# Moving the output stores of an attention kernel from SyncE's DMA queue to ScalarE's

## The chip, the cores and the metric

The kernel runs on one core of a Trainium2 chip. A core has five engines that run side by side and meet at semaphores: TensorE (matrix products), VectorE, ScalarE (activation functions such as exp), GpSimd and SyncE. Data moves between the chip's memory (HBM) and the on-chip memory (SBUF) by DMA, which the core's 16 DMA engines carry out. SyncE and ScalarE can each start transfers on a DMA queue of their own.

The metric is the time of one execution on the device in microseconds (us). Before the change it is 831.01 us, the median of three runs from 830.96 to 833.51 us.

## The reference

The kernel computes attention with a full softmax over 16 x 32 = 512 heads, each with 192 queries, 1024 keys and a head size of 128, in bf16:

```python
B, H, Sq, Sk, D = 16, 32, 192, 1024, 128
def reference(q, k, v):
    scale = q.shape[-1] ** -0.5
    scores = jnp.einsum("bhqd,bhkd->bhqk", q, k) * scale
    p = _softmax(scores, axis=-1)
    return jnp.einsum("bhqk,bhkd->bhqd", p, v)
```

The inputs are normal numbers times 0.05. K and V are 134 MB each, Q and the output 25 MB each.

## The kernel before, in words

**Groups and fills.** Four heads make a group x, of which there are NQ = 128. The scores of a group are worked on in three fills, so there are NF = 384 fills; fill f is part b = f mod 3 of group x = f // 3. In a fill TensorE makes transposed scores of all four heads into PSUM (`qk`, line 616): one bank for one head (`f_s2`) and a set of three banks for the other three (`f_s0` and `f_s1` in turn). ScalarE takes the exp of the one bank (line 782) and of the three (line 785), and writes bf16 probabilities to `f_pt`. The maximum isn't subtracted. The sum of the exps comes from a column of ones next to V.

**P times V.** Four fills later (LAG = 4) TensorE multiplies the probabilities by V (`pv`, line 638) into one PSUM bank, `f_o`. On VectorE `onorm` takes the reciprocal of the sums (line 722, which counts up the semaphore `s_rc`) and multiplies by it (line 726), which writes a third of a group's output to `f_ob`. As `f_o` is a single bank, the next `pv` waits for that multiplication (semaphore `s_on`).

**Loads.** For each group SyncE starts a load of V (line 517, 1024 KB), of K (line 503, 1024 KB) and of Q (line 509, 192 KB). There are five buffers of each. K and Q are transposed on VectorE (lines 701 and 710) and K is put in order on GpSimd (line 573); V is copied on GpSimd to lie beside its ones (line 582). A load of K waits until VectorE has transposed the group that had its buffer; a load of V waits for the P·V step past which its buffer is free.

**Stores.** The output of two groups is stored by one transfer of 384 KB in pieces of 768 B (line 529); the last two groups have one each. That makes 65 stores. The buffer `f_ob` has NSO = 3 slots of two groups, and VectorE's first multiplication into a slot waits until the slot's last store has landed (semaphores `s_st`). A store waits for the reciprocal after its last block's multiplication, which tells that the block is written.

**The order on SyncE.** The whole order is written out by hand in one loop over n: load V of group n+3, K and Q of group n+5, and then, for every second n, one store. SyncE works through it in order, so a store that has to wait holds back the loads behind it, and a load that has to wait, for its buffer or for room in the queue, holds back the store.

**ScalarE.** Its loop over the fills holds nothing but the waits and the two exps of each fill.

**A second path.** Behind the main path follows a general path that runs only if a check of the sums, made at the end, asks for it. It isn't entered with these inputs and is left as it is.

Of the kernel before, what the change touches and what calls it, by code (L numbers as in the profile page):

```python
# [408 lines left out]
def _attention_kernel(nc, q, k, v, out):  # L409
# [4 lines left out]
    NQ = NH // 4  # L414
# [4 lines left out]
    NF = 3 * NQ  # L419
# [4 lines left out]
    NSO = 3  # L424
# [5 lines left out]
    of = out.rearrange("b h s d -> (b h) s d")  # L430

    stores = [(x, GQ) for x in range(0, NQ - GQ, GQ)] + [(NQ - 2, 1), (NQ - 1, 1)]
    EARLY = NF - 9

    with ExitStack() as outer:
        redo = outer.enter_context(nc.sbuf_tensor("redo", [1, 1], mybir.dt.int32))

        def sem(name):
            return outer.enter_context(nc.semaphore(name))
# [7 lines left out]
        s_st = [sem("f_st%d" % i) for i in range(NSO)]  # L447
# [9 lines left out]
        s_rc = sem("f_rc")  # L457
        s_pf = sem("f_pf")
        s_on = sem("f_on")
        s_fin = sem("f_fin")  # L460
        s_fl = sem("f_fl")

        with ExitStack() as es:
            def sb(name, shape, dt):
                return es.enter_context(nc.sbuf_tensor(name, shape, dt))
# [16 lines left out]
            ob = sb("f_ob", [128, NSO, GQ * 6, D], BF16)  # L482
# [10 lines left out]
            def o_of(s):  # L493
                if NF - 4 <= s < NF - 1:
                    return s3_ps[0][:, s - (NF - 4), :].rearrange("p (u c) -> p u c", u=2)
                return o_ps[:]

            @block.sync
            def _(e):
                def load_k(x):  # L500
                    if x >= NKN:
                        e.wait_ge(s_kx, 3 * (x - NKN) + 3)
                    e.dma_start(
                        kn[:, x % NKN, :],
                        kf[4 * x:4 * x + 4].rearrange("a (j r) d -> (a j) (r d)", r=32).bitcast(U32),
                    ).then_inc(s_kn[x % NKN], 16)

                def load_q(x):
                    e.dma_start(
                        qn[:, x % NKN, :],  # L510
                        qf[4 * x:4 * x + 4].rearrange("a (j u) d -> (a j) (u d)", u=6).bitcast(U32),
                    ).then_inc(s_qn[x % NKN], 16)

                def load_v(x):
                    if x >= NVS:
                        e.wait_ge(s_pv, 3 * (x - NVS) + 2 + BLANK)
                    e.dma_start(
                        vs[:, x % NVS, :, :],
                        vf[4 * x:4 * x + 4].rearrange("a (m t) d -> m a (t d)", t=T),
                    ).then_inc(s_v[x % NVS], 16)  # L520

                def store(i):
                    so = i % NSO
                    x, c = stores[i]
                    if x + c == NQ:
                        e.wait_ge(s_fin, 1)
                    else:
                        e.wait_ge(s_rc, 3 * (x + c) + 1)
                    e.dma_start(
                        of[4 * x:4 * x + 4 * c].rearrange("(a x) (p j) d -> (x p) a (j d)", x=2, j=3),  # L530
                        ob[:, so, 0:6 * c, :].rearrange("p (a j) d -> p a (j d)", j=3),
                    ).then_inc(s_st[so], 16)

                k0 = kf[0:4].rearrange("a (j s t) d -> (a j) s (t d)", s=4, t=8).bitcast(U32)
                kn0 = kn[:, 0].rearrange("p (s w) -> p s w", s=4)
                cut = 32 * PIECES[0][1]
                e.dma_start(kn0[:, :, 0:cut], k0[:, :, 0:cut]).then_inc(s_k0, 16)
                load_q(0)
                e.dma_start(kn0[:, :, cut:], k0[:, :, cut:]).then_inc(s_kn[0], 16)
                load_k(1)  # L540
                load_q(1)
                for n in range(2, NKN):
                    load_v(n - 2)
                    load_k(n)
                    load_q(n)
                si = 0
                for n in range(NQ + 3):
                    if n + NKN - 2 < NQ:
                        load_v(n + NKN - 2)
                    if n + NKN < NQ:  # L550
                        load_k(n + NKN)
                        load_q(n + NKN)
                    if si < len(stores) - 2 and n >= sum(stores[si]) + 2:
                        store(si)
                        si += 1
                while si < len(stores):
                    store(si)
                    si += 1
                for so in range(NSO):
                    e.wait_ge(s_st[so], 16 * len(range(so, len(stores), NSO)))  # L560

# [209 lines left out]
            @block.scalar  # L771
            def _(act):
                act.wait_ge(s_one, 1)
                act.activation(pt[:, 1].rearrange("p a c -> p (a c)").bitcast(F32), ones[:, 0:1].to_broadcast([128, 2 * T * SQ]),  # L774
                               ACT_FN.Copy).then_inc(s_set, 1)
                for f in range(NF):
                    x, b = divmod(f, 3)
                    act.wait_ge(s_qk, f + 1)
                    if 0 < 3 * x + b and b < 2:
                        act.wait_ge(s_pv, 3 * (x - R) + 2 + b + BLANK)  # L780
                    c = slice(512 * b, 512 * b + 512)
                    act.activation(pt[:, x % R, 0, c], s1_ps[:], ACT_FN.Exp, scale=scale).then_inc(s_e1, 1)  # L782
                    if b == 0:
                        act.wait_ge(s_pf, x + 1)
                    act.activation(pt[:, x % R, 1:4, c], s3_ps[f % 2][:], ACT_FN.Exp, scale=scale).then_inc(s_e3, 1)  # L785

        _general_path(nc, q, k, v, out, redo)


def bass_standalone__mha_softmax__near_ridge_kernel(  # L790
    nc: bass.Bass,
    q: bass.AP,
    k: bass.AP,
    v: bass.AP,
    out: bass.AP,
):
    _attention_kernel(nc, q, k, v, out)
# [28 lines left out]
```

## Time and profile before

| Quantity | Value |
|---|---|
| time, median of 3 runs | 831.01 us |
| span of the profiled execution | 829.9 us |
| TensorE busy | 810.1 us (98%) |
| ScalarE busy | 748.5 us (90%), 384 exps of 1444 ns and 384 of 597 ns |
| VectorE busy | 601.8 us (73%) |
| GpSimd busy | 550.9 us (66%) |
| DMA | 319.21 MB, 385 GB/s over the span |
| time of the packets on SyncE's queue, share of 16 DMA engines | 100.6% |
| stores, from issue to landing (median) | 13.8 us |
| loads of K, V, Q, from issue to landing (median) | 14.2, 12.5, 12.9 us |

The profile is one execution seen by the hardware profiler. PE stands for TensorE, DVE for VectorE, ACT for ScalarE, POOL for GpSimd, SPq for the issuing of SyncE. An issue is the time in which the issuing engine hands a transfer over; its landing is when the data has arrived and the semaphore is up. In the timelines a line gives the start in us, the length in us, the engine, the line of the program and the operation, and in square brackets the idle time ahead of it with what ended it. Matmuls are pipelined, so a busy TensorE says only that it had work at all times.

### The profile page before, as it was taken

Reading aid. Unit: us, or ns where it says so; the run is one execution under the profiler, and the core shown is the slowest. Engines: PE = TensorE matmul, PEld = TensorE weight load, DVE = VectorE, ACT = ScalarE, POOL = GpSimd, SP = SyncE. Lnnn points to the kernel's source line nnn. Section 1 sums busy time; section 2 is a strip of 40 time slices with the busy share of each in tenths; the row PEclk is TensorE's granted clock in tenths of the full one; section 3 lists DMA queues with packets and bytes.
Section 4 is the critical chain, followed back from the end, with each engine's and each line's share of the span. In section 5 each row is a group of like instructions: output and inputs, shape, how many; then the busy total and the mean of one; then the engine's idle time right before and its main releaser. Section 6 shows DMA issues by size and latency. Waiting matters only on the chain. (4 is left out here: it accounts for less than half of the span.)

```text
span 829.9 us, 71554 instructions
## 1 busy us (share of the span) xinstructions
PE 810.1 (98%) x32926; PEld 718.3 (87%) x32926; DVE 601.8 (73%) x1288; ACT 748.5 (90%) x770; POOL 550.9 (66%) x646
## 2 busy tenths in 40 slices
PE   6899999999999999999999999999999999999995
PEld 4788888888888888888888888888888888888885
DVE  5477777777777777777777777777777777777763
ACT  5699999999999999999999999999989999999994
POOL 6566766766766766766766666666766666666671
PEclk9899999999999999999999999999999999999999
DMA  8999999999999999999999999999999999999981
GB/s 323 399 403 399 406 403 401 406 403 402 405 403 404 402 400 389 399 382 374 398 400 398 376 399 395 388 400 405 387 383 399 406 397 397 387 393 405 399 323 46
DMA packets 139214, 319.21 MB, mean 385 GB/s; under 512 B 7201, under 2 KB 57377, under 8 KB 122913
## 3 DMA queue, kind: packets, MB, share of 16 engines
q1 hardware_dynamic: 139168, 318.80, 100.6%
q14 instruction: 40, 0.32, 0.1%
q8 instruction: 6, 0.10, 0.1%
HBM read 293.60 MB, written 25.17 MB: 384 GB/s over the span
## 5 line engine op out<-in xcount | busy, mean ns | idle before, releaser
L785 ACT ACTIVATE f_pt<-f_s 128x1536 bf16<-128x1536 f32 x384 | 554.5, 1444 | 3.4 <-PE f_o L638 3.4
L573 POOL COPY f_kt<-f_kx 128x768 uint32<-128x768 uint32 (+1 forms) x384 | 294.2, 785 | 258.1 <-DVE f_kx L701 139.8
L638 PE MATMUL f_o<-f_vp,f_pt 128*64 128x129 bf16 x12336 | 424.9, 222 | 5.2 <-issue 3.3
L616 PE MATMUL f_s<-f_qt,f_kt 32*128 32x192 bf16 (+2 forms) x20480 | 422.2, 226 | 5.0 <-issue 3.2
L638 PEld LDWEIGHTS f_o<-f_vp,f_pt 128*64 128x64 bf16 x12336 | 366.1, 110 | 57.6 <-issue 28.3
L616 PEld LDWEIGHTS f_s<-f_qt,f_kt 32*128 32x128 bf16 x20480 | 347.8, 92 | 41.2 <-issue 5.5
L701 DVE STREAM_TRANSPOSE f_kx<-f_kn 128x768 uint32<-128x768 uint32 (+1 forms) x384 | 334.7, 872 | 32.0 <-DMA f_kn<-in_k_dram 30.2
L782 ACT ACTIVATE f_pt<-f_s 128x512 bf16<-128x512 f32 x384 | 229.3, 597 | 65.7 <-PE f_s L616 38.1
L582 POOL COPY f_vp<-f_vs 128x1024 uint32<-128x1024 uint32 x256 | 259.9, 1044 | 5.9 <-PE f_o L638 5.5
L722 DVE RECIPROCAL f_rinv<-f_o 128x2 f32<-128x2 f32 x381 | 64.3, 169 | 166.3 <-PE f_o L638 165.8
L726 DVE TENSOR_TENSOR f_ob<-f_o,f_rinv 128x256 bf16<-128x256 f32 x381 | 161.8, 425 | 19.7 <-DMA out_dram<-f_ob 7.1
L710 DVE STREAM_TRANSPOSE f_qt<-f_qn 128x384 uint32<-128x384 uint32 x128 | 72.9, 569 | 0.0
L663 PE MATMUL f_o<-f_ones 128*128 128x512 bf16 x12 | 5.3, 632 | 1.1 <-POOL f_ones L564 1.1
L663 PEld LDWEIGHTS f_o<-f_ones 128*128 128x128 bf16 x12 | 1.6, 144 | 3.8 <-issue 2.8
L565 POOL MEMSET f_vp<- 128x4352 uint32 x1 | 3.7, 3730 | 0.0
L682 DVE MEMSET f_pt<- 128x3072 uint32 x1 | 2.6, 2618 | 1.5 <-PEq L811 1.5
L638 PE MATMUL f_s<-f_vp,f_pt 128*64 128x129 bf16 x96 | 3.1, 220 | 0.3 <-PEq L599 0.3
L638 PEld LDWEIGHTS f_s<-f_vp,f_pt 128*64 128x64 bf16 x96 | 2.8, 110 | 0.5 <-issue 0.5
L774 ACT ACTIVATE f_pt<-f_ones 128x3072 f32<-128x3072 bf16 x1 | 2.8, 2762 | 0.0
L774 ACT ACT_TABLE_LOAD x1 | 1.3, 1283 | 0.8 <-PEq L811 0.8
L722 DVE RECIPROCAL f_rinv<-f_s 128x2 f32<-128x2 f32 x3 | 0.5, 170 | 1.4 <-PE f_s L638 1.4
L676 PE MATMUL f_o<-f_bad,f_ones 128*1 128x1 bf16 x1 | 0.2, 164 | 1.3 <-DVEq L766 1.3
(13 smaller groups left out, 5.3 us busy)
## 6 DMA issues: line engine op xcount, KB each, us to landing
f_vs<-in_v_dram SPq DMA_DIRECT2D x128, 1024.0 KB, 12.5
f_kn<-in_k_dram SPq DMA_DIRECT2D x127, 1024.0 KB, 14.2
f_qn<-in_q_dram SPq DMA_DIRECT2D x128, 192.0 KB, 12.9
out_dram<-f_ob SPq DMA_DIRECT2D x63, 384.0 KB, 13.8
f_kn<-in_k_dram SPq DMA_DIRECT2D x1, 640.0 KB, 6.6
f_kn<-in_k_dram SPq DMA_DIRECT2D x1, 384.0 KB, 4.0
out_dram<-f_ob SPq DMA_DIRECT2D x2, 192.0 KB, 2.0
```

The source lines that it names most:

```text
L573: gp.tensor_copy(kt[:, x % NKT].bitcast(U32).rearrange("p U (j s u) c -> p U j s (u c)", s=2, u=2)[:, lo:hi], kx[:, x % 2].rearrange("p (U ...
L582: gp.tensor_copy(vp[:, x % NVP, 2 * T * i: 2 * T * i + 2 * T, 0:D].bitcast(U32), vs[:, x % NVS, 2 * i: 2 * i + 2, :].rearrange("p a (t d) ...
L616: ins = pe.matmul(S[:, c0: c0 + n1 - n0], kt[r, x % NKT, 2 * t + h, :, c], qt[r, x % R, h, n0:n1, c], start=w == 0 and g == 0, stop=w == 3 ...
L638: return pe.matmul(O[m0: m0 + m, u, 0:129], pt[:, x % R, 2 * y + z, t * SQ + n0: t * SQ + n0 + m], vp[:, x % NVP, (2 * y + z) * T + t, 0:129],
L663: pe.matmul(o_ps[:].rearrange("p a b -> p (a b)"), ones[:], ones[:].unsqueeze(1).to_broadcast([128, 4, 128]), start=True, stop=True)
L701: dve.transpose(kx[:, x % 2].rearrange("p (U s j u) -> p s u U j", s=2, j=32, u=2)[:, :, :, lo:hi], kn[:, x % NKN].rearrange("p (s u U i) ...
L710: dve.transpose(qt[:, x % R].bitcast(U32).rearrange("p b (y j u) c -> p u y b (j c)", y=3, u=2), qn[:, x % NKN].rearrange("p (u y b i) -> ...
L722: dve.reciprocal(ri, O[:, :, 128]).then_inc(s_rc, 1)
L726: dve.tensor_tensor(ob[:, so, 6 * a + 2 * w: 6 * a + 2 * w + 2, :], O[:, :, 0:128], ri.unsqueeze(2).to_broadcast([128, 2, D]), ALU.mult,). ...
L774: act.activation(pt[:, 1].rearrange("p a c -> p (a c)").bitcast(F32), ones[:, 0:1].to_broadcast([128, 2 * T * SQ]), ACT_FN.Copy).then_inc( ...
L782: act.activation(pt[:, x % R, 0, c], s1_ps[:], ACT_FN.Exp, scale=scale).then_inc(s_e1, 1)
L785: act.activation(pt[:, x % R, 1:4, c], s3_ps[f % 2][:], ACT_FN.Exp, scale=scale).then_inc(s_e3, 1)
```

## The change

The function that starts a store moves out of SyncE's block, so that either engine can call it. ScalarE calls it right behind the second exp of fill 3(x+c)+6, where x is the first group of the store and c its number of groups. The last block of that store is block 3(x+c)-1, whose P·V product TensorE makes right after the scores of fill 3(x+c)+3; the reciprocal that the store waits for belongs to the following block, a fill later. The exp is two fills past that. Stores for which this fill doesn't exist, the last three, stay on SyncE, behind all its loads. SyncE's loop then holds loads only. The waits, the sizes and the slots stay as they were.

The change is meant to take the waits of stores out of the order of the loads, and the wait for a load's buffer out of the way of the stores.

```diff
+            def store(e, i):
+                so = i % NSO
+                x, c = stores[i]
+                if x + c == NQ:
+                    e.wait_ge(s_fin, 1)
+                else:
+                    e.wait_ge(s_rc, 3 * (x + c) + 1)
+                e.dma_start(
+                    of[4 * x:4 * x + 4 * c].rearrange("(a x) (p j) d -> (x p) a (j d)", x=2, j=3),
+                    ob[:, so, 0:6 * c, :].rearrange("p (a j) d -> p a (j d)", j=3),
+                ).then_inc(s_st[so], 16)
+
+            store_at = {3 * (x + c) + 6: i for i, (x, c) in enumerate(stores) if 3 * (x + c) + 6 < NF}
...
             @block.sync
...
-                si = 0
-                for n in range(NQ + 3):
+                for n in range(NQ):
                     if n + NKN - 2 < NQ:
                         load_v(n + NKN - 2)
                     if n + NKN < NQ:
                         load_k(n + NKN)
                         load_q(n + NKN)
-                    if si < len(stores) - 2 and n >= sum(stores[si]) + 2:
-                        store(si)
-                        si += 1
-                while si < len(stores):
-                    store(si)
-                    si += 1
+                for i in range(len(store_at), len(stores)):
+                    store(e, i)
...
             @block.scalar
...
                     act.activation(pt[:, x % R, 1:4, c], s3_ps[f % 2][:], ACT_FN.Exp, scale=scale).then_inc(s_e3, 1)
+                    if f in store_at:
+                        store(act, store_at[f])
```

More of the change, by code (lines that the diff above doesn't have):

```diff
@@ L520, in load_v @@
                     ).then_inc(s_v[x % NVS], 16)
[L522 to L532, printed above, removed]
                 k0 = kf[0:4].rearrange("a (j s t) d -> (a j) s (t d)", s=4, t=8).bitcast(U32)
```

## The prediction

> **What bounds the kernel now.** I read the page's shares first, then busy time by stretch, then the list of waits, and last the timelines of ScalarE, VectorE, TensorE and SyncE.
>
> The busy times by stretch (columns: busy time of PE, weight loads, DVE, ACT, POOL with counts, then clock, share of the DMA engines, GB/s):
>
> ```profile
> 45.00:535.00 490.00, 489.99 (x20206) 436.81 (x20204) 366.37 (x790) 458.80 (x474) 337.02 (x395) 1.00 1.04 397
> 535.00:800.00 265.00, 263.17 (x10792) 233.99 (x10782) 197.27 (x422) 244.87 (x254) 179.62 (x211) 1.00 1.04 396
> ```
>
> TensorE has no gap in the first stretch and 1.8 us of gaps in the second. The DMA engines are full in both. So two bounds lie almost on each other. In the ScalarE timeline the starts of L782 are 12.42 us apart over six fills (two groups of four heads), in every such stretch from fill 12 (44.72 us) to fill 252 (541.72 us) but two, and those lose 0.1 us each. From there on they are 12.45 to 13.13 us apart. Against fill by fill medians of the early part, fills 252 to 380 lose 3.5 us in all, and 3.0 of it falls on fills whose number leaves 5 when divided by 6: once per pair of groups, the rhythm of a store. What happens there, at its worst (start, length, engine, line):
>
> ```profile
> 600.38 2.24 SPq L529 DMA_DIRECT2D out_dram<-f_ob  x1
> 602.42 0.42 DVE L726 TENSOR_TENSOR f_ob<-f_o,f_rinv 128x256 bf16<-128x256 f32 x1 [0.86 <-DMA out_dram<-f_ob]
> 602.99 1.10 PE L638 MATMUL f_o<-f_vp,f_pt 128*64 128x129 bf16 x32 [0.61 <-PEq L599]
> 605.17 0.60 ACT L782 ACTIVATE f_pt<-f_s 128x512 bf16<-128x512 f32 x1 [0.81 <-PE f_s L616]
> ```
>
> VectorE wants to write an output slot whose previous store has not landed. It waits 0.86 us; TensorE's next P·V waits 0.61 us for the single output bank; the exp after it comes late. In the list of waits this is the second line:
>
> ```profile
> DVE f_kx L701 <- DMA f_kn<-in_k_dram: 30.2, 42, 3.6
> DVE f_ob L726 <- DMA out_dram<-f_ob: 7.1, 22, 0.9
> ```
>
> (us in total, how often, the longest). 6.7 us of the 7.1 lie between 535 and 800 us. K waits are there too, 17.6 us in 32 waits of at most 0.8 us:
>
> ```profile
> 544.08 0.98 DVE L701 STREAM_TRANSPOSE f_kx<-f_kn 128x768 uint32<-128x768 uint32 x1 [0.72 <-DMA f_kn<-in_k_dram]
> 544.98 0.13 DVE L722 RECIPROCAL f_rinv<-f_o 128x2 f32<-128x2 f32 x1
> ```
>
> They lengthen no fill yet, but the reciprocal behind this one shows no idle time, where it usually has some 0.55 us. VectorE's slack is used up by a K wait of 0.7 us.
>
> **Why late and not early.** SyncE issues every transfer, in order:
>
> ```profile
> 66.47 0.17 DVE L722 RECIPROCAL f_rinv<-f_o 128x2 f32<-128x2 f32 x1 [0.58 <-PE f_o L638]
> 70.64 0.55 SPq L529 DMA_DIRECT2D out_dram<-f_ob  x1
> 74.72 0.38 SPq L517 DMA_DIRECT2D f_vs<-in_v_dram  x1
> ...
> 501.48 3.47 SPq L517 DMA_DIRECT2D f_vs<-in_v_dram  x1
> 505.00 4.38 SPq L503 DMA_DIRECT2D f_kn<-in_k_dram  x1
> 509.41 0.43 SPq L509 DMA_DIRECT2D f_qn<-in_q_dram  x1
> ```
>
> At 71.19 us it has nothing to do for 3.5 us; at 500 us one issue follows on the other and some last over 4 us: the queue takes no more. Summing SyncE's gaps ahead of V loads over 0.2 us gives 38 us for 45 to 150, 13 us for 250 to 350 and none after 450. The lead melts because supply is below demand. A group needs 1024 + 1024 + 192 KB of loads and 192 KB of stores, 2.49 MB, in 6.21 us: 401 GB/s, against 397 supplied. The packet records of the trace show why: [...]768 B of a store in 36 ns, 2 KB of V in 86, 8 KB of K in 316 ns before 150 us and 336 between 350 and 535.
>
> **What the Trainium skill says.** "DMA: Bandwidth & Descriptors", section "Issuing engines are not separate DMA queues": transfers started by different engines run on the same 16 DMA engines and only issue time is saved. The trace agrees as far as it goes: the one queue already fills the engines (1.04). The same page, "Queues, rings and completion order": each DMA engine takes packets round robin from the rings that have work; so a store on a second ring overtakes queued loads. No run here shows it yet. "Perfetto Trace Analysis", section "DMA Instruction — HWDGE (DVE, Sync)": the descriptor generator is locked for one issuing engine until its descriptors are made, and others wait for the lock. The trace has one issuer, so it cannot show that. "Advanced Engine Details and Errata", section "Sequencer Loop": other engine instructions can be queued while a control instruction runs. That is what would hide an issue behind an exp; not shown here either.
>
> **The change, part by part.**
> 1. *62 of 65 stores leave SyncE.* The rule for the fill is 3(x+c)+6 < 384, so ends x+c = 2 to 124. SyncE saves 62 x 0.45 us = 28 us of issuing and the waits for the reciprocal (8.1 us between 150 and 535). It is worth nothing by itself: where SyncE has gaps nobody waits for it, and where it has none it waits for the DMA queue.
> 2. *62 issues on ScalarE.* An unhindered issue takes 0.43 us (median of the 231 SyncE issues under 0.7 us). Its semaphore wait is long over: the store in fill 186, whose first exp starts at 405.00 us, needs the reciprocal that ended at 402.08. Behind the issue is queued L782 of the next fill. ScalarE sends L785 off at 405.49, that exp lasts 1.44 us, and L782 starts at 407.05. So between 0 (hidden behind L785) and 62 x 0.43 = 27 us (if all of it came after the exp). ScalarE has only 0.12 to 0.17 us between L785 and the next L782, so what isn't hidden reaches TensorE. I take 0: 0.43 us fits three times into the exp.
> 3. *The stores land sooner.* Today 13.8 us from issue, the whole queue ahead. On its own ring at most about 32 packets an engine, each next to one load packet: 32 x (36 + 86) ns = 3.9 us beside V, 32 x (36 + 316) = 11.3 us beside K. From fill X+6 to the reuse of the slot at the P·V step X+12 are some ten fills, 20.7 us. The slot wait ends: 3.0 us of lost fills fall away.
> 4. *The bytes stay.* Without the slot waits TensorE asks for 401 GB/s where 397 came. Over the 265 us that is 265 x (401/397 - 1) = 2.7 us of lateness, and K has next to no slack left. If DMA stays exactly as quick, K waits take back up to 2.7 of the 3.0 us (gain 0.3 us: 830.7). If queue depth freed of stores carries the loads over the dips, all 3.0 stay (828.0). I take the middle, a gain of 1.5 us: **829.5 us**.
> 5. *The end.* The last three stores and the chain behind the last P·V stay on SyncE as they are: nothing.
>
> **The rivals.**
> - *TensorE alone bounds* (0.20): two rings interleave small store packets with the loads and the 8 KB packets keep their early 316 ns. Packets over 400 ns cost 12 us per engine over the run, so there is room. Then 371 fills after fill 12 take 371 x 2.07 = 768.0 instead of 771.7 us: 831.0 - 3.7 = 827.3. This is the floor, as the change leaves TensorE's work alone. For: early supply was 403. Against: nothing shown says that a second ring helps.
> - *ScalarE waits for the descriptor generator* (0.19): the issue comes while SyncE holds it. Laid over the SyncE timeline of before, 12 of the 62 places fall more than 1.5 us ahead of the end of a SyncE issue; the overhang is 29 us. Each stall slows the demand and lets SyncE out of its jam, so I estimate a third to a half: 831 - 1.5 + 12 = 841 us, at worst 860. For: SyncE is issuing for 722 us of the span. Against: a separate queue may have its own room.
> - *The mix makes DMA slower* (0.13): with 1% less, 745 us need 401/393 - 1 = 2.0% more, 15.2 us, less the lead that lasted until 540 (0.9% of 490 us = 4.3 us) gives 10.9 us of stalls instead of 3.5: 838 us.
> - The forecast has 0.48: K takes over from the slot, 828.0 to 830.7.
>
> **How the numbers follow.** A change of 0.3% is 2.5 us, so faster means below 828.5. The forecast gives 0.13 faster and 0.33 same, and 0.02 slower; the first rival 0.20 faster; the other two give 0.03 same (stalls that nearly vanish) and 0.29 slower. That is 0.33 faster, 0.36 same, 0.31 slower. The range starts at 827.0, just below the floor, and ends at 841, which takes in the slow rivals' middles and leaves out their tails, about 0.15.
>
> **What would show it.** In the changed profile: the row of DVE L726 waiting for the output store gone (part 3); stores landing in 4 to 12 us; ScalarE's idle ahead of L782 in store fills still 0.12 to 0.17 us (part 2), or over 1 us if the generator is shared; K waits of VectorE above 17.6 us after 535 us and fills lengthened at a K load instead of at every sixth (part 4); GB/s between 45 and 535 above or below 397 for the first and third rivals. I am wrong if ScalarE shows issue records of several us beside SyncE's, or if the mix of rings changes the time of a K packet by over 1%.

## The result, and the profile after

The changed kernel takes 827.61 us (median of 4 runs, 827.07 to 827.89) against 831.65 us for the kernel before in the same session (830.96 to 833.51; a fourth run moved its median from 831.01). The ratio is 0.9947, with a 95% interval from 0.9928 to 0.9966: half a per cent faster, and the runs lie closer together. Over all sessions single runs of the kernel before reach from 828.0 to 840.3 us, so some of them lose nothing; each trace below shows one execution.

Busy time by stretch in the changed kernel (columns as before: us, PE, weight loads, DVE, ACT, POOL, clock, share of the DMA engines, GB/s):

```profile
45.00:535.00 490.00, 489.96 (x20208) 436.76 (x20202) 365.96 (x790) 458.76 (x474) 337.05 (x395) 1.00 1.04 404
535.00:800.00 265.00, 265.00 (x10942) 236.20 (x10928) 198.11 (x428) 248.16 (x257) 181.75 (x213) 1.00 1.01 390
```

TensorE has no gap left after 535 us, where it had 1.8 us. The DMA engines brought 404 GB/s where they brought 397. The 390 of the second stretch is no lack: the loads ran ahead and were through earlier, which is why the engines' share falls to 1.01. From the 13th exp to the last, TensorE's floor of 371 fills x 2.07 us = 768.0 us was overrun by 3.7 us before and is overrun by 0.2 us now. So the time went to the floor that the first rival had named.

The list of waits of the changed kernel for 45 to 800 us; this line is all in it that names `f_kn` or `f_ob` (us in total, how often, longest):

```profile
DVE f_ob L724 <- DVE f_rinv L720: 0.3, 1, 0.3
```

It is a wait for the reciprocal, not for a transfer. The wait for the output slot is gone, and so are the waits for K, of which 17.6 us stood after 535 us alone.

SyncE's timeline at the place shown before (start, length, engine, line):

```profile
68.31 0.38 SPq L532 DMA_DIRECT2D f_vs<-in_v_dram  x1
68.73 0.65 SPq L518 DMA_DIRECT2D f_kn<-in_k_dram  x1
69.42 0.43 SPq L524 DMA_DIRECT2D f_qn<-in_q_dram  x1
74.53 0.38 SPq L532 DMA_DIRECT2D f_vs<-in_v_dram  x1
```

SyncE is free for 4.7 us between its turns, and it stays so: its issue records add up to 212 us, against 701 us before. ScalarE's timeline, at the place of a store:

```profile
504.17 0.60 ACT L780 ACTIVATE f_pt<-f_s 128x512 bf16<-128x512 f32 x1
504.58 0.38 ACTq L505 DMA_DIRECT2D out_dram<-f_ob  x1
504.66 1.44 ACT L783 ACTIVATE f_pt<-f_s 128x1536 bf16<-128x1536 f32 x1
506.24 0.60 ACT L780 ACTIVATE f_pt<-f_s 128x512 bf16<-128x512 f32 x1
```

The issue lies beside the exps: L783, which stands ahead of it in the program, starts while it is made. The next L780 starts 2.07 us after the last, as in fills without a store. The stores land 9.5 us after their issue in the median (13.8 before). The page's list of queues shows the second one (packets, MB, share of the 16 engines):

```profile
q1 hardware_dynamic: 106432, 294.41, 91.0%
q10 hardware_dynamic: 32736, 24.38, 8.8%
```

**Where the supply came from.** The bytes are the same, but the packets took less time: 99.8% of 826.2 us for the two queues together against 100.6% of 829.9 us for the one, some 10 us less per engine. The packet records of the two traces, means in ns between 45 and 790 us:

| packet | per engine and group | before | after |
|---|---|---|---|
| 8 KB of K | 8 | 326.2 | 314.8 |
| 2 KB of V | 32 | 86.1 | 86.3 |
| 1.5 KB of Q | 8 | 66.0 | 65.2 |
| 768 B of a store | 16 | 36.3 | 36.1 |
| sum, with the semaphore writes | | 6504 | 6412 |
| divided by the engines' share, 1.037 | | 6273 | 6184 |

The share is the packets' summed time over the time of 16 engines in these 745 us; it is over 1, so the records overlap a little. TensorE needs a group every 6210 ns. Before, the DMA engines took 63 ns too long for a group; now they are 26 ns ahead, and with the share between 45 and 535 us, 1.039, it would be some 40 ns. K packets alone make the difference. In the trace before they are slow in every second load. Counted off in order of their start, 128 to a load, they take 333 ns in the mean from group 10 on against 319. The packets of neighbouring loads mix in time, so these two means are blurred, and the 337 and 316 ns named in run 7's expectation don't come out in this way; which load is slower does. It is the last K load ahead of the store in SyncE's queue, with only Q between them.

The line divided by the share needs care. It is close to 745 us over the groups moved in them, so it is the rate that was reached and doesn't by itself say what set it. That the DMA engines set it before is read from VectorE's waits for K (19.4 us between 45 and 800 us, none after).

### The profile page after: what moved, and what is told of

The parts are those of the page before. It is cut to its first block, busy times and chain, and to the rows that moved or that the text cites. A ratio compares the mean times of both kernels' runs of the same rounds, so it can differ in the third digit from the quotient of the medians.

```text
span 826.2 us, 71554 instructions
## 1 busy us (share of the span) xinstructions
PE 807.5 (98%) x32926; PEld 717.1 (87%) x32926; DVE 599.8 (73%) x1288; ACT 748.5 (91%) x770; POOL 550.4 (67%) x646
## 5 line engine op out<-in xcount | busy, mean ns | idle before, releaser
L783 ACT ACTIVATE f_pt<-f_s 128x1536 bf16<-128x1536 f32 x384 | 554.6, 1444 | 3.3 <-PE f_o L636 3.3
L780 ACT ACTIVATE f_pt<-f_s 128x512 bf16<-128x512 f32 x384 | 229.3, 597 | 62.0 <-PE f_s L614 32.3
```

## The experiments

All ratios are against the kernel before, run beside them on the same chip; its median was 831.3 to 832.9 us there. "K packets" and "V packets" are the means of the 8 KB and 2 KB packets between 45 and 790 us, in the one execution that was traced.

**1. Only the slot wait taken away.** Stores stay on SyncE.

```diff
-    NSO = 3
+    NSO = 5
```

> Stores stay on SyncE; five output slots instead of three, so that a store may land two slots later before VectorE waits for it. Slot theory (the only loss was the wait for an output slot): that wait goes and the time falls to the floor, 827.5 us. Supply theories (the DMA engines supplied 397 GB/s where TensorE needs 401, and the change raised that supply): the slot wait goes, but VectorE's waits for K after 535 us grow from 17.6 us and lengthen fills instead; 830 to 831 us, and the mean 8 KB packet of K stays near 326 ns between 45 and 790 us (315 ns in the changed kernel).

Measured: 833.92 us, ratio 1.0003 (0.9978 to 1.0027). The list of waits after 535 us has no line for the output slot any more. Instead, from that list and from the stretches:

```profile
DVE f_kx L701 <- DMA f_kn<-in_k_dram: 27.1, 40, 1.9
ACT f_pt L782 <- PE f_s L616: 14.1, 61, 1.3
```

```profile
45.00:535.00 490.00, 489.81 (x20191) 436.78 (x20181) 366.20 (x788) 458.53 (x475) 335.56 (x395) 1.00 1.04 396
535.00:800.00 265.00, 261.44 (x10721) 232.33 (x10719) 194.72 (x419) 243.02 (x251) 178.46 (x210) 1.00 1.03 394
```

K waits rose from 17.6 to 27.1 us and TensorE lost 3.6 us after 535 us. K packets stayed slow, 328.1 ns. This is the most telling run: the wait that the profile named was real, and taking it away alone is worth nothing (the interval leaves room for a gain of 0.2%, not for the 0.5% of the change), because the next wait for the same scarce thing stood behind it.

**2. A shorter queue.** Four buffers of K, Q and V; stores on SyncE.

```diff
-    NKN, NVS, NKT, NVP = 5, 5, 2, 2
+    NKN, NVS, NKT, NVP = 4, 4, 2, 2
```

> Stores stay on SyncE; four buffers of K, Q and V instead of five, so that fewer loads are under way and SyncE's queue is never full. Jam theory (a full queue on SyncE goes with slow K packets; the change took the store packets, 32 per engine, out of that queue): issues on SyncE stay under 1.5 us, K packets fall to about 315 ns, and the time falls below 829 us in spite of the smaller lead. Mix theory (a second ring beside the loads is what makes K packets quicker): K packets stay at 326 ns or more, and with less lead the time is 831 us or more.

Measured: 830.15 us, ratio 0.9968 (0.9951 to 0.9985); K packets 318.1 ns; SyncE's issues add up to 419 us, but 15 of them still last over 4 us, so the queue is full less often and not never. Some gain, between the two theories. The slow loads are now those of the other parity (322 against 314 ns, counted off as above), and with four buffers it is a load of that parity that stands ahead of the store. So the slowness goes with the place in the queue and not with the group.

**3. A full queue without stores in it.** The changed kernel with six buffers.

```diff
-    NKN, NVS, NKT, NVP = 5, 5, 2, 2
+    NKN, NVS, NKT, NVP = 6, 6, 2, 2
```

> The changed kernel (stores on ScalarE) with six buffers of K, Q and V instead of five: more loads under way. Jam theory: SyncE's queue fills up again although no store is in it, issues of 4 us come back, K packets rise above 322 ns and the time goes to 828.5 us or more (a larger lead may hide some of it). Mix theory: K packets stay at 315 ns, the time at 827.5 us.

Measured: 828.24 us, ratio 0.9946 (0.9923 to 0.9969); K packets 316.4 ns. SyncE's timeline:

```profile
500.57 4.86 SPq L518 DMA_DIRECT2D f_kn<-in_k_dram  x1
505.47 0.95 SPq L524 DMA_DIRECT2D f_qn<-in_q_dram  x1
506.46 0.86 SPq L532 DMA_DIRECT2D f_vs<-in_v_dram  x1
507.37 4.40 SPq L518 DMA_DIRECT2D f_kn<-in_k_dram  x1
```

and the store on ScalarE's in the middle of the first of these:

```profile
504.62 0.38 ACTq L505 DMA_DIRECT2D out_dram<-f_ob  x1
```

Two theories fall here. SyncE's issues add up to 763 us of 826, and the kernel still runs at the floor: a full queue costs nothing by itself. And 60 of ScalarE's 62 issues start in the midst of an issue of SyncE, yet they take 378 ns in the median and 444 ns at most: nothing shared holds ScalarE up by more than some 70 ns.

**4. A second ring without the stores on it.** Q from group 5 on is loaded by ScalarE, behind the second exp of fill 3x; stores stay on SyncE.

```diff
                         load_k(n + NKN)
-                        load_q(n + NKN)
...
                     act.activation(pt[:, x % R, 1:4, c], s3_ps[f % 2][:], ACT_FN.Exp, scale=scale).then_inc(s_e3, 1)
+                    if b == 0 and x + NKN < NQ:
+                        act.wait_ge(s_kx, 3 * x + 3)
+                        act.dma_start(
...
+                        ).then_inc(s_qn[(x + NKN) % NKN], 16)
```

> Stores stay on SyncE; the loads of Q (from group 5 on, 192 KB each, 8 packets per engine and group) are issued by ScalarE behind the second exp of fill 3x. A second ring exists, with small packets, but the store packets stay in SyncE's queue. Mix theory: K packets near 315 ns and 827.5 us. Jam theory: SyncE's queue carries 112 packets per engine and pair of groups instead of 128 (96 in the changed kernel), so the jam is milder, not gone: K packets 318 to 324 ns and 828.5 to 830.5 us. Issuing theory: 123 issues of 0.38 us on ScalarE lie behind the exps and cost nothing.

Measured: 834.24 us, ratio 1.0023 (1.0000 to 1.0045); K packets 326.4 ns. Two rings as such don't help: the time didn't fall, with the small packets of Q on the second one.

**5. A store on ScalarE too early.**

```diff
-            store_at = {3 * (x + c) + 6: i for i, (x, c) in enumerate(stores) if 3 * (x + c) + 6 < NF}
+            store_at = {3 * (x + c) + 3: i for i, (x, c) in enumerate(stores) if 3 * (x + c) + 6 < NF}
```

> The changed kernel with each store of ScalarE behind the exp of fill 3(x+c)+3 instead of 3(x+c)+6, so that its wait is not yet over: the reciprocal it waits for comes after the P.V product that follows the scores of the next fill. Hidden-issue theory (an issue on ScalarE is free only because its wait is long over): ScalarE stands some 1.5 us per store, 62 x 1.5 = 93 us, so 905 to 930 us. If the exps could pass a waiting issue: 827.6 us.

Measured: 923.30 us, ratio 1.1088 (1.1042 to 1.1133): 95.7 us over the changed kernel, 1.54 us per store. ScalarE's timeline at a store, and the line of the waits:

```profile
499.35 1.44 ACT L783 ACTIVATE f_pt<-f_s 128x1536 bf16<-128x1536 f32 x1
502.17 0.38 ACTq L505 DMA_DIRECT2D out_dram<-f_ob  x1
502.65 0.60 ACT L780 ACTIVATE f_pt<-f_s 128x512 bf16<-128x512 f32 x1 [1.86 <-DVE f_rinv L720]
```

```profile
ACT f_pt L780 <- DVE f_rinv L720: 116.6, 62, 2.2
```

The exp cannot pass the waiting issue. "Two fills past" is what makes the change possible: three fills earlier the same line of code costs 11%.

This run shows one thing more. Its last stretch:

```profile
535.00:800.00 265.00, 236.89 (x9716) 210.52 (x9710) 175.70 (x380) 219.36 (x228) 162.09 (x190) 1.00 1.00 357
```

ScalarE sets the pace here and 357 GB/s are asked for, yet the DMA engines' share is still 1.00, and packets are long (K 327.9, V 99.0 ns) with no store among the loads. So a share near 1 doesn't show by itself that the DMA engines bound, and packet times of a run in which another engine stands still don't compare with the others.

**6. Twice as many issues on ScalarE.** A store per group, six slots of one group.

```diff
-    GQ = 2
-    NSO = 3
+    GQ = 1
+    NSO = 6
...
-    stores = [(x, GQ) for x in range(0, NQ - GQ, GQ)] + [(NQ - 2, 1), (NQ - 1, 1)]
+    stores = [(x, GQ) for x in range(0, NQ - 2, GQ)] + [(NQ - 2, 1), (NQ - 1, 1)]
```

> The changed kernel with a store for every group instead of every second one (192 KB each, six slots of one group, the same memory): 125 issues on ScalarE instead of 62. Hidden issues: 827.5 us, ScalarE's idle ahead of the next exp still 0.12 to 0.17 us. If an issue takes exp time, half of 0.38 us for each of 63 more would give 839 us. K packets 315 ns in either case.

Measured: 827.96 us, ratio 0.9938 (0.9916 to 0.9960), with 125 issues of 378 ns on ScalarE and K packets at 311.3 ns. An issue whose wait is over is free here.

**7. A store per group on SyncE.** The same edit in the kernel before.

> The kernel before with a store for every group (192 KB, six slots of one group), all on SyncE. The slow K loads of the kernel before are every second one, the one directly ahead of the store in SyncE's queue (337 against 316 ns per packet). Neighbour theory (a K load with store packets behind it in the same queue is slow): now every K load has a store behind it, half as large; odd and even K loads become alike, near 326 ns, and the time stays at 830 to 834 us. Jam theory (only the room that a large store takes matters): the queue fills more evenly, K packets fall below 320 ns and the time below 829.5 us.

Measured: 827.85 us, ratio 0.9942 (0.9921 to 0.9963). K packets 315.5 ns, alike in both parities (315.3 and 315.8). The stretches:

```profile
45.00:535.00 490.00, 489.99 (x20210) 436.75 (x20206) 366.04 (x790) 458.83 (x474) 337.10 (x395) 1.00 1.04 404
535.00:800.00 265.00, 264.98 (x10932) 236.19 (x10928) 198.00 (x428) 248.10 (x256) 181.81 (x213) 1.00 1.02 392
```

This is the whole gain without the second queue, with all stores in SyncE's queue and SyncE's issues adding up to 764 us. The neighbour theory, as put, is wrong too: a K load with a smaller store behind it isn't slow.

**8. The store at another place in SyncE's order.** Between V and K instead of behind Q.

```diff
+                    if si < len(stores) - 2 and n >= sum(stores[si]) + 2:
+                        store(si)
+                        si += 1
                     if n + NKN < NQ:
                         load_k(n + NKN)
                         load_q(n + NKN)
-                    if si < len(stores) - 2 and n >= sum(stores[si]) + 2:
-                        store(si)
-                        si += 1
```

> The kernel before with the store issued between V and K of its turn (V, store, K, Q) instead of behind Q. Neighbour theory: the slow K load is now not followed by a store (Q and V of the next turn lie between); K packets fall to about 316 ns in both parities and the time to 828 us. Jam theory: the same packets in the same queue, K packets stay near 326 ns in the mean and the time at 830 to 834 us, perhaps with the slow load in the other parity.

Measured: 830.46 us, ratio 0.9974 (0.9954 to 0.9995), 21 of 22 runs from 828.27 to 835.98. K packets 317.2 ns, but V packets 88.0 instead of 86.1: in this trace part of the loss lies in V, which neither theory had.

**9. Small stores, but two at once.** As run 7, but in every second turn, at the old place.

```diff
-                    if si < len(stores) - 2 and n >= sum(stores[si]) + 2:
+                    while n % 2 == 0 and si < len(stores) - 2 and n >= sum(stores[si]) + 2:
```

> Stores of one group each (192 KB, six slots) on SyncE, but issued two at a time in every second turn, at the place of the store in the kernel before. Lump theory (384 KB of store packets in one piece in the load queue every second group make the K loads come in an uneven rhythm, every second one slow): as the kernel before, 831 to 834 us, K packets of the two parities 316 and over 330 ns. Size theory (smaller transfers on SyncE are what helped the run with a store per turn): 827.9 us, parities alike.

Measured: 828.48 us, ratio 0.9966 (0.9953 to 0.9979); K packets 314.8 ns in the mean, 316.0 and 313.4 by parity. The stretches:

```profile
45.00:535.00 490.00, 490.00 (x20212) 436.78 (x20206) 366.03 (x790) 458.92 (x474) 337.20 (x395) 1.00 1.04 402
535.00:800.00 265.00, 264.99 (x10936) 236.26 (x10928) 198.24 (x428) 248.07 (x257) 181.87 (x213) 1.00 1.03 395
```

So it isn't the lump of 384 KB every second turn; it is that it is *one* transfer. Nor does the gain come from what the change was meant for, to take the waits of stores out of the order of the loads: in this run stores hold SyncE for 121.9 us between 45 and 800 us, where it was 15.8 us in the kernel before, and the gain is there. The smaller slots that come with the smaller stores aren't it either, as run 1 took the slot wait away for nothing.

**10 and 11. Stores of four groups, 768 KB,** two slots of four groups, on SyncE and on ScalarE.

```diff
-    GQ = 2
-    NSO = 3
+    GQ = 4
+    NSO = 2
...
-    stores = [(x, GQ) for x in range(0, NQ - GQ, GQ)] + [(NQ - 2, 1), (NQ - 1, 1)]
+    stores = [(x, GQ) for x in range(0, NQ - GQ, GQ)] + [(NQ - 4, 2), (NQ - 2, 1), (NQ - 1, 1)]
```

> The kernel before with a store for every four groups (768 KB, two slots of four groups), on SyncE: the lump is twice as large and half as frequent. Lump theory: as slow as the kernel before or slower, 832 to 838 us, the K load directly ahead of the store the slowest of four. Otherwise: no different from the kernel before.

> The changed kernel with a store for every four groups (768 KB, two slots of four groups), on ScalarE. If the second queue spreads any lump among the loads: 827.6 to 828.5 us and K packets under 318 ns. If the lump works on the second queue too: K packets over 322 ns and 829 us or more.

Measured on SyncE: 835.14 us, ratio 1.0035 (1.0021 to 1.0049). The time is as foretold, the reason isn't: K packets are at 315.9 ns, and V packets at 90.1. Its two waits:

```profile
DVE f_kx L701 <- DMA f_kn<-in_k_dram: 24.4, 34, 3.0
DVE f_ob L726 <- DMA out_dram<-f_ob: 9.9, 15, 1.3
```

Both waits of the kernel before are back. On ScalarE: 828.44 us, ratio 0.9962 (0.9948 to 0.9977), K packets 315.7 and V packets 86.7 ns. On its own queue the size made no difference to the time.

**12. The changed kernel once more,** beside runs 9 to 11.

> The changed kernel as it is, beside the others on one chip: 827.6 us, K packets 315 ns; the measure for the runs with other stores on ScalarE and for the store per group on SyncE (827.85 us).

Measured: 828.18 us, ratio 0.9956 (0.9941 to 0.9970), K packets 315.1 ns. No version went clearly below it: runs 3, 6, 7, 9 and 11 lie within 0.9 us of the first measurement, all at TensorE's floor.

Put together, by size of one store transfer:

| one store | on SyncE, in the load queue | on ScalarE |
|---|---|---|
| 192 KB | 827.85 us; packets 6196 ns per group | 827.96 us; 6173 ns |
| 384 KB | 831.3 to 832.9 us (the kernel before); 6273 ns | 828.18 us; 6186 ns |
| 768 KB | 835.14 us; 6313 ns | 828.44 us; 6190 ns |

The times in ns are worked out as in the table above, each with its own share (1.037 to 1.039). Every row keeps to this: over 6210 VectorE waits for K and the time is above the floor, under it neither is so. The line isn't sharp, though. Runs 2, 8, 4 and 1 come to 6244, 6262, 6268 and 6296 ns, and their traced executions overran the floor by 2.1, 3.2, 4.5 and 6.0 us (the kernel before, at 6273, by 3.7). But run 9 comes to 6227 and lost 0.1 us. A shortfall of 17 ns in 120 groups is 2.0 us, less than the 4.3 us of lead that the prediction had worked out; so in run 9 the lead lasts to the end (an estimate from these numbers).

## Why the prediction was right or wrong

The time, 827.61 us, lies in the range and below the 829.5 us named; the case that came true was the first rival, given 0.20, and not the forecast. That the time lay inside is owed to the width of the range, 827.0 to 841, which took in the rivals. The 829.5 was the middle of two cases, and the gain was 4.0 us where it said 1.5.

**Part 1, SyncE's issues are worth nothing by themselves: right.** SyncE stopped being full, but runs 3 and 7 reach the floor with SyncE's issues adding up to 763 and 764 us. (For the kernel before the records add up to 701 us, not to the prediction's 722.)

**Part 2, an issue on ScalarE is hidden: right,** at 0.38 us instead of 0.43. Run 6 doubles the issues for nothing. Run 5 shows the condition: 1.54 us each when the wait is open. The Trainium skill's section "Sequencer Loop" in "Advanced Engine Details and Errata" agrees in this: exps run on while an issue is made.

**Part 3, the slot wait ends: right,** with landings of 5.6 to 11.2 us for 61 of the 62 stores, inside the 4 to 12 us named, and 2.6 us for the last, when the loads were over. Its 3.0 us of gain, though, wasn't the slot's to give: run 1 ended that wait and gained nothing.

**Part 4, "The bytes stay": this step failed.** Its condition, DMA "exactly as quick", was taken as the likeliest and didn't hold. Where the condition holds, the step does: in run 1 the slot wait goes, K waits take its place and nothing is gained (ratio 1.0003; the step had said 0.3 us). But with the change the DMA engines brought more: per group 6184 ns instead of 6273, just below the 6210 that TensorE needs. The 2.7 us of lateness became none, and all of the 3.5 us came back. The margin is thin: 0.4%. The prediction had named this as a sign of being wrong, a K packet's time changed by over 1%: it fell by 3.5%. Its other way to the full gain, queue depth freed of stores, isn't what did it: run 7 has the gain with the stores in the queue.

**The first rival** was right in time and in what it looked at, the K packets over 400 ns. Over the whole trace these took 11.6 us per engine more than at 316 ns each before, and 2.5 us after. Its reason, that two rings interleave small packets with the loads, is neither enough nor needed: run 4 has two rings and slow K packets, run 7 has one ring and quick ones. How the second ring keeps a large store from slowing the loads isn't shown.

**The second rival, ScalarE waiting for the descriptor generator, is refuted** by run 3: 444 ns at most, with SyncE in an issue at 60 of 62. The Trainium skill, "Perfetto Trace Analysis", section "DMA Instruction — HWDGE (DVE, Sync)", says that an issuing engine waits while another holds the generator. Here no such wait shows between SyncE and ScalarE; the measurement decides. (The traces don't tell in which part of a long issue SyncE would hold the generator.)

**The third rival** had the right quantity and the wrong sign.

**What stays open.** That a store of 384 KB or more in one transfer among the loads costs time is shown by many runs of each version (runs 7, 9 and 10 against the kernel before). That it does so by slower packets of the loads rests on one trace of each, and run 5 warns that packets can also be long for another reason. Why they are slower is not shown. It isn't the room in the queue (run 3), a second ring (run 4), the bytes per turn (run 9) or the load's being next to a store (run 7). The loss sits in K packets at 384 KB and in V packets at 768 KB. One transfer of 384 KB and two of 192 differ, among other things, in the order in which the rows of the output are written and in the number of store packets per engine up to the semaphore write, 32 or 16; neither was tried as the cause. Nor is it known why some runs of the kernel before lose nothing.

## What to carry to other kernels

When the profile names one wait for a transfer and the DMA engines are full, work out packet time per unit of work against the bounding engine's time: removing the named wait moves the loss to the next one, as in run 1, unless that sum falls. Make sure of "full" by the waits for loads: in run 5 the engines' share was 1.00 and ScalarE was the bound. A transfer on a busy compute engine's queue is free if its semaphore is long up and longer work is under way, and dear if not (0 against 1.54 us each here). Before taking a second queue, try smaller transfers in the first: here both gave the same half per cent.

## What the runs showed of the hardware that was not expected

- The time of an 8 KB packet into SBUF isn't fixed: half of those of K take 309 ns or less in the changed kernel, and the mean is 311.3 to 316.4 ns in all versions with 192 KB stores or with stores on ScalarE at the right place, but 326.2 to 328.1 ns with five buffers of loads and a 384 KB store behind them in the same queue (the kernel before, runs 1 and 4). In run 5, where ScalarE stands still at each store, it is 327.9 ns without them.
- The engines' summed packet time can be 1.00 of theirs at 357 GB/s with another engine as the bound (run 5), where it is 1.04 at 404 GB/s in the first stretch of the changed kernel.
- A large store in the load queue costs more than two halves issued one after the other at the same place: 831.3 against 828.48 us on one chip.
- The issue of a store on ScalarE takes 378 ns in the median whether the transfer is 192, 384 or 768 KB (runs 6, 12 and 11), and in run 3 it took 378 ns while SyncE was in an issue of 4.86 us.
